# A first scatter pass for expert 0 alone, ahead of the full pass, in a fused attention and two-MoE kernel

## The chip, the cores and the metric

The kernel runs on one core of one Trainium2 chip. The metric is the device time of one execution in microseconds (us). The kernel before takes 1359.37 us, the median of three runs (1359.05 to 1359.9).

A core has five engines that run their own instruction streams: TensorE (PE) multiplies matrices, VectorE (DVE) and ScalarE (ACT) work on tiles elementwise, GpSimd (POOL) issues the indirect DMAs here, and SyncE (SP) issues the plain DMAs. "SPq" and "POOLq" in a profile are the parts of SP and POOL that issue DMAs. The core's 16 DMA engines move the data.

## The reference, cut to what matters

```python
def reference(**kwargs):
    attn_out = _attn_ref(...)          # windowed attention, 2 x 8 heads x 768 x 64
    x = attn_out.transpose(0, 2, 1, 3).reshape(1536, 512)
    x = _moe_ref(x=x, **moe_kwargs)    # every token through all 8 experts, soft weights
    return _moe2_ref(x=x, **moe2_kwargs)

def _moe2_ref(x, w_gate, w1, w2):
    cap = N // E                       # 1536 // 8 = 192
    logits = x @ w_gate
    for idx in np.argsort(-logits.flatten()):
        tok, e = idx // E, idx % E     # a token goes to the best expert that has room
        if assigned[tok] >= 0 or counts[e] >= cap: continue
        assigned[tok] = e; counts[e] += 1
    for e in range(E):
        mask = assigned == e           # exactly 192 tokens
        h = np.maximum(x[mask] @ w1[e], 0.0)
        out[mask] = h @ w2[e]
```

The case is about the passage from the first MoE to the second. Once the assignment is known, each expert of the second MoE needs its own 192 token rows, which lie scattered over the 1536 rows of the first MoE's result.

## The kernel before, in words

**Tokens.** The 1536 tokens stand in 12 tiles of 128. The first MoE's result lies in `acc[0]` to `acc[5]`, two tiles each. The last tiles to be finished are 10 and 11: their sums (`accl` in the profile) close only with the last matmuls of the first MoE (`make_g2`, L1163), while the routing is already known for all tokens.

**Routing to rows.** `pos[:, t]` says for each token of tile t which row it gets in the DRAM array `xs_d`: rows 0 to 191 are expert 0's, 192 to 383 expert 1's and so on. `scatter(t)` (L2056) writes a tile's 128 rows of 513 numbers there with an indirect DMA from POOL. Tiles 0 to 9 (NE = 10) are scattered as soon as the rows are known (L1950). Tiles 10 and 11 follow in `make_last_scatters` (L1955), after expert 0's rows were read.

**Fetch.** `make_rows` has SP read each expert's 192 rows back into `xs` (L2100): expert 0's once the first ten scatters have landed, the others' once all twelve have.

**Expert 0.** Its rows from tiles 10 and 11 are not in `xs_d` yet when it is read. They come by another way: DVE builds a one-hot table per tile (`hot`, from an IOTA named `slot` and the positions), and TensorE multiplies `accl` by it (`direct`, L2174), straight into a PSUM bank. Onto the same bank it adds the rows that were fetched, by fp32 matmuls with the identity (`move`, L2165). For the other experts the rows are turned by transposes (`tr`, L2150). ACT then copies the bank to `xe` in fp32r (the high part, L2154), DVE subtracts and keeps the low part (L2158).

**Steps.** The second MoE has 64 steps, eight for each expert (u = 0 to 3 blocks of 256 hidden columns, two halves each). A step is m1 (L2211 and L2213: four pairs of matmuls, hidden activations), a PSUM read by ACT and an add by DVE, the split `hs` into high and low part (ACT L2233, DVE L2237), and m2 (L2255 to L2264: five matmuls onto the expert's output banks). The weights arrive by SP in halves, `w1r` (L938) and `w2r` (L943), and are split into `w1hs`/`w1ls` and `w2hs`/`w2ls` (ACT L962, DVE L960). There are four weight slots, so expert 1's block u reuses the slot of expert 0's block.

**Order.** A list scheduler at build time fixes the order of instructions on each engine. A task has an engine, a planned duration, predecessors and a priority; among those that could start soon the one of lowest priority goes first. Where the planner sees TensorE idle, `warm` fills the gap with transposes of the identity (L206). Each engine then runs its list strictly in order, and waits where its next instruction is not ready.

Of the kernel before, what the change touches and what calls it, by code (L numbers as in the profile page):

```python
# [22 lines left out]
def tile_attention_moe_moe(ctx, tc, q, k, v, n_sink, window, wg1, w1a, w2a, wg2, w1b, w2b, out):  # L23
# [5 lines left out]
    P = 128  # L29
# [35 lines left out]
    class Task:  # L65
        __slots__ = ("alts", "fn", "deps", "prio", "acq", "rel", "left", "succ", "end", "eng", "closed", "name")
# [18 lines left out]
    class Sched:  # L85
# [11 lines left out]
        def task(self, eng, cost, fn, deps=(), prio=0.0, use=(), acq=None, rel=None, name=""):  # L97
            x = Task()
            x.name = name
            x.alts = [(eng, cost)] if isinstance(eng, str) else list(zip(eng, cost))  # L100
            x.fn, x.prio, x.acq, x.rel, x.succ, x.end, x.eng = fn, prio, acq, rel, [], None, None
# [109 lines left out]
        def emit(self, x, eng, t, cost):  # L211
# [14 lines left out]
            if len(x.alts) > 1:  # L226
                x.fn(eng)
            else:
                x.fn()
# [697 lines left out]
    def make_load(n):  # L927
# [18 lines left out]
        def load(k):  # L946
# [3 lines left out]
            return task("SP", 1.46, l2, deps=deps + [d1] + (SCT[NE - 1:NE] if 1 <= need - n_defer < 3 else []), prio=pr - 21, use=hs_[1:], name=f"raw{n}")  # L950
# [193 lines left out]
    def make_g2(s, hh_, hd, pr, what, jo=0, dyn=False):  # L1144
# [20 lines left out]
        for j in range(GT):  # L1165
            oh = [] if dyn else [OH_[jo + j]]
            for parts in ((0,), (1,), (2,)) if dyn else ((0, 1, 2),):
                y = task("PE", 0.2325 * len(parts), lambda j=j, parts=parts: g2(j, parts),
                         deps=hd + [LAST.get(("g2", jo + j)), FREE.get(f"o{jo + j}")] + w2t[f], prio=pr,
# [346 lines left out]
    def make_gate2():  # L1516
# [23 lines left out]
        def zero_rows(j):  # L1540
            nc.sync.dma_start(xs_d[j * P:(j + 1) * P, :], gp["zero"])
# [6 lines left out]
        for j in range(NT):  # L1548
            ZR.append(task("SP", 1.5, lambda j=j: zero_rows(j), deps=[x], prio=pr + 8.0 * j))
# [94 lines left out]
    def make_parts(s, g, fc, hh_, pr):  # L1644
# [8 lines left out]
        return a, task(("DVE", "POOL"), (0.43, PLO), lo, deps=[a], prio=pr, use=[hh_], name="hlo")  # L1653
# [3 lines left out]
    def make_deferred(q_):  # L1657
# [11 lines left out]
        a, b = make_parts(s, g, fc, hh_, pr - 32.5)  # L1669
        DEF.extend((a, b))  # L1670
        make_g2(s, hh_, [a, b], pr + 5.0, (LE, g, n, f, k == 0, k == 2 * NU - 1), dyn=True)
# [21 lines left out]
    def make_routing():  # L1693
# [256 lines left out]
        for t in range(NE):  # L1950
            SCT.append(task("POOL", 1.1, lambda t=t: scatter(t), deps=[place_, CB[t]] + ZR, prio=t, name="scatter"))
# [3 lines left out]
    def make_last_scatters():  # L1955
        for t in range(NE, NT):
            SCT.append(task("POOL", 1.1, lambda t=t: scatter(t), deps=[placed, CB[t]] + LDX[0], prio=t, name="scatter"))
# [96 lines left out]
    sc, SCT = [], []  # L2054

    def scatter(t):  # L2056
        nc.gpsimd.memset(spacer, 0.0)
        i = nc.gpsimd.indirect_dma_start(
            out=xs_d[:, :], out_offset=bass.IndirectOffsetOnAxis(ap=pos[:, t:t + 1], axis=0),
            in_=acc[t // GT][:, t % GT, :], in_offset=None)  # L2060
        for o in sc:
            tc.declare_no_dep(i.ins, o.ins, reason="distinct rows")
        sc.append(i)
# [11 lines left out]
    XS, XE, IDX, rkp, oh = {}, {}, {}, {}, {}  # L2075
# [15 lines left out]
    def make_rows(e, sw):  # L2091
# [5 lines left out]
        def ldx():  # L2097
            for n, (o, m) in enumerate(parts_of(e)):
                x = rkp["p"].tile([P, XW], F32, name=f"xs{n}", bufs=3)[:m]
                nc.sync.dma_start(x[:, :w], xs_d[e * cap + o:e * cap + o + m, :w])  # L2100
                XS[e, n] = x

        LDX[e].append(task("SP", 1.1, ldx, deps=SCT + [sw, placed], prio=v_two(8 * e - 26.0) - (500 if e == 0 else 0), use=[XSH[e]], name=f"xs{e}"))

    def make_tr(e):
# [14 lines left out]
        if e == 0:  # L2120
# [4 lines left out]
            ARR = [task("X", 4.0, lambda: None, deps=LDX[0], name="landed")]  # L2125
# [14 lines left out]
        for c2 in range(DC // 2):  # L2140
# [19 lines left out]
            def move(c2=c2, key=key):  # L2160
                p = bank[key][:, :2 * cap].rearrange("p (a b) -> p a b", a=2)
                for cc in range(2):
                    c = 2 * c2 + cc
                    for n, (o, m) in enumerate(parts):
                        nc.tensor.matmul(p[:, cc, o:o + m], XS[e, n][:, c * P:(c + 1) * P], ident[:m, :m],  # L2165
                                         start=False, stop=(cc == 1 and n == 1), skip_group_check=True)

            def direct(t, c2=c2, key=key):
                if c2 == 0 and t == NE:
                    XE[e] = rkp["p"].tile([P, DC, 2, cap], F32R, name="xe")  # L2170
# [251 lines left out]
```

## Time and profile before

| | |
|---|---|
| median of three runs | 1359.37 us (1359.05 to 1359.9) |
| the profiled execution | 1360.64 us |
| its span, first to last instruction | 1358.7 us |
| PE busy | 1348.2 us, 99% |
| DVE, ACT, POOL busy | 915.8, 607.2, 95.4 us |
| granted TensorE clock, mean | 0.998 of full speed |
| last matmuls of the first MoE | 1187.67 us |
| first m1 of the second MoE | 1196.22 us |

Times in the profile count from the first instruction of one profiled execution. That execution took 1360.64 us, 1.94 us longer than its span. Matmuls are pipelined: the start of the next one is the better mark than a duration, and "x4" after a row means four like it in a run. In square brackets stands how long the engine was idle just before, and what ended the wait.

### The profile page before, as it was taken

What the parts mean: (1) busy time and instruction counts of PE and PEld (TensorE: products, weight loads), DVE (VectorE), ACT (ScalarE), POOL (GpSimd) and SP (SyncE); (2) the same over time, 40 slices, a digit from 0 to 9 for tenths busy, and PEclk for the clock granted to TensorE, in tenths of its full rate; (3) what the DMA queues carried; (4) which work ended last, traced back from release to release, by engine and by line L of the source; (5) the groups of instructions that cost most, each with busy time, mean ns of one, the idle gap of its engine ahead of it and who ended that gap; (6) DMA issues with size and microseconds to landing.
All of it is one profiled execution on the core that took longest, in us unless ns stands there. A gap on an engine that the chain in (4) does not pass through costs nothing.

```text
span 1358.7 us, 22466 instructions
## 1 busy us (share of the span) xinstructions
PE 1348.2 (99%) x8288; PEld 1169.6 (86%) x8288; DVE 915.8 (67%) x2438; ACT 607.2 (45%) x1536; POOL 95.4 (7%) x246
## 2 busy tenths in 40 slices
PE   9999999999999999999999999999999999999997
PEld 7988888989989888899988899888887777788886
DVE  7877757865555555646364645459889868678885
ACT  7766653734333332424242433231133454367774
POOL 3111110000000000000000000000001013410111
PEclk9999999999999999999999999999999999999999
DMA  8331111202010101111020201064020011378873
GB/s 181 97 75 42 40 31 41 78 17 63 16 48 17 47 21 44 31 32 49 14 63 1 62 1 63 16 213 129 16 80 30 1 32 47 96 234 278 245 234 91
DMA packets 100036, 99.02 MB, mean 73 GB/s; under 512 B 42248, under 2 KB 76552, under 8 KB 99792
## 3 DMA queue, kind: packets, MB, share of 16 engines
q1 hardware_dynamic: 97936, 91.22, 22.9%
q0 software_dynamic: 1984, 6.30, 1.3%
q8 instruction: 67, 1.10, 0.3%
q14 instruction: 49, 0.40, 0.1%
HBM read 86.47 MB, written 11.04 MB: 72 GB/s over the span
## 4 chain that ended last, share of the span: by engine, by line
PE 96%; DMA 1%; DVE 1%; POOL 1%; issue 0%; ACT 0%; POOLq 0%; ACTq 0%; SPq 0%
PE hp L1381 16%; PE o L1470 12%; PE hp L1228 10%; PE o L1163 9%; PE side L1381 6%; PE av L1470 6%; PE side L1470 6%; PE hp L1132 5%; PE side L1163 2%; PE av L754 2%; PE av L1163 2%; PE side L731 1%; PE side L2211 1%; PE o L206 1%; PE hp L2211 1%; PE side L507 1%
## 5 line engine op out<-in xcount | busy, mean ns | idle before, releaser
L1439 ACT ACTIVATE hh<-c 128x256 fp32r<-128x256 f32 x180 | 74.8, 415 | 124.3 <-DVE c L1406 110.5
L1228 PE MATMUL hp<-xp,w1hs 128*128 128x512 f32 x384 | 120.7, 395 | 0.0
L1406 DVE TENSOR_TENSOR c<-hp,cp 128x256 f32<-128x256 f32 x120 | 50.9, 424 | 96.5 <-PE hp L1381 92.5
L1470 PE MATMUL o<-w2ls,hh 128*128 128x512 f32 x240 | 94.5, 394 | 0.0
L1470 PE MATMUL o<-w2hs,hl 128*128 128x512 f32 x240 | 94.5, 394 | 0.0
L1470 PE MATMUL o<-w2hs,hh 128*128 128x512 f32 x240 | 94.4, 393 | 0.0
L1381 PE MATMUL hp<-xp,w1hs 128*128 128x256 f32 x480 | 88.6, 282 | 0.0
L1228 PEld LDWEIGHTS hp<-xp,w1hs 128*128 128x128 f32 x384 | 69.5, 188 | 14.9
L1442 DVE SCALAR_TENSOR_TENSOR hl<-c,hh 128x256 fp32r<-128x256 f32 x180 | 74.5, 419 | 10.4 <-ACT hh L1439 7.9
L1381 PEld LDWEIGHTS hp<-xp,w1hs 128*128 128x128 f32 x480 | 76.8, 188 | 4.4
L1228 PE MATMUL hp<-xp,w1ls 128*128 128x512 f32 x192 | 75.8, 395 | 0.0
L1132 PE MATMUL hp<-xp,w1hs 128*128 128x256 f32 x384 | 75.5, 289 | 0.0
L1163 PE MATMUL o<-w2hs,hh 128*128 128x512 f32 x176 | 71.5, 406 | 0.0
L1439 ACT ACTIVATE hh<-hp 128x256 fp32r<-128x256 f32 x60 | 23.0, 384 | 107.4 <-PE hp L1381 107.4
L1163 PE MATMUL o<-w2hs,hl 128*128 128x512 f32 x176 | 69.6, 395 | 0.0
L1163 PE MATMUL o<-w2ls,hh 128*128 128x512 f32 x176 | 69.4, 394 | 0.0
L1398 ACT ACTIVATE cu<-hp 128x256 f32<-128x256 f32 x60 | 23.1, 385 | 103.1 <-PE hp L1381 103.0
L1381 PE MATMUL hp<-xp,w1ls 128*128 128x256 f32 x240 | 67.4, 281 | 0.0
L1442 DVE SCALAR_TENSOR_TENSOR hl<-hp,hh 128x256 fp32r<-128x256 f32 x60 | 25.5, 425 | 58.6 <-ACT hh L1439 58.3
L960 DVE TENSOR_TENSOR w1ls<-w1r,w1hs 128x512 fp32r<-128x512 f32 x84 | 56.8, 684 | 11.2 <-ACT w1hs L962 10.8
L1132 PEld LDWEIGHTS hp<-xp,w1hs 128*128 128x128 f32 x384 | 60.4, 189 | 2.5 <-DVE xp L787 0.2
L1248 ACT ACTIVATE hh<-hp 128x256 fp32r<-128x256 f32 x48 | 16.8, 383 | 98.0 <-PE hp L1228 96.5
(512 smaller groups left out, 3976.9 us busy)
## 6 DMA issues: line engine op xcount, KB each, us to landing
wr<-in_moe_w_dram SPq DMA_DIRECT2D x44, 512.0 KB
w1r<-in_moe_w_dram SPq DMA_DIRECT2D x42, 512.0 KB
w2r<-in_moe_w_dram SPq DMA_DIRECT2D x42, 512.0 KB
xs<-xs_d SPq DMA_DIRECT2D x14, 256.5 KB
xs_d<-zero SPq DMA_DIRECT2D x12, 256.5 KB
nk<-in_k_dram SPq DMA_DIRECT2D x12, 256.0 KB
nq<-in_q_dram SPq DMA_DIRECT2D x12, 256.0 KB
nv<-in_v_dram SPq DMA_DIRECT2D x12, 256.0 KB
```

What stands on the lines that cost most here:

```text
L754: nc.tensor.matmul(o[hh * D:(hh + 1) * D, hp, :], NAT["v", bl[j]][:, 2 * hp + hh, :], ET[t, hp][:, hh, j, :], start=(hp == 0 and z < 2), s ...
L960: (nc.gpsimd if eng == "POOL" else nc.vector).tensor_tensor(lo[:, c], r[:, c], f32(hi[:, c]), op=OP.subtract)
L1132: nc.tensor.matmul(p, a, b, start=(c == 0 and j == 0), stop=(c == DC - 1 and j == 2), skip_group_check=True)
L1163: nc.tensor.matmul(OUTP[g, j], a_, b_, start=(first and i == 0), stop=(last and i == 2), skip_group_check=True)
L1228: nc.tensor.matmul(HS[k, 0].rearrange("p a b -> p (a b)"), a, b, start=(c == 0 and j == 0), stop=(c == DC - 1 and j == 2), skip_group_chec ...
L1381: nc.tensor.matmul(st[bk], l_[:, c], r_[:, c], start=(start and c == 0 and j == 0), stop=(c == 1 and j == 2), skip_group_check=True)
L1398: act(st[key], st[bk], AF.Copy)
L1406: tt(st[out], st[bk], st[key], op=OP.add)
L1439: act(hh, st[key], AF.Relu)
L1442: nc.vector.scalar_tensor_tensor(HT[i, f, t][1], st[key], 0.0, f32(HT[i, f, t][0]), op0=OP.max, op1=OP.subtract)
L1470: nc.tensor.matmul(OUTP[g, j % GT], a_, b_, start=(first and f == 0 and z == 0), stop=(last and f == 1 and z == 2), skip_group_check=True)
L2211: nc.tensor.matmul(p[:, :2 * cap], h1[:, w], XE[e][:, c].rearrange("p s t -> p (s t)"), start=(c == 0), stop=False, skip_group_check=True)
```

## The change

Expert 0 gets a DRAM array of its own, `xs0_d` of 192 rows. POOL first scatters tiles 0 to 9 with a bound: rows of 192 and above are dropped, so that only expert 0's rows are written. Only then does the full pass over tiles 0 to 9 into `xs_d` follow, and tiles 10 and 11 after it, which no longer wait for a read. Expert 0's fetch waits for the first pass alone; the fetches of the other experts wait for the full pass as before.

On TensorE, expert 0's `direct` products keep banks of their own. ACT copies them to SBUF (`keep`), the rows fetched are turned by transposes instead of identity matmuls, DVE adds the two (`join`), and ACT and DVE make high and low part from the sum.

Smaller edits: two more zero writes for `xs0_d`; the early `w2r` loads that waited for the ten scatters now wait for the first pass; the last ten low-part subtractions of the first MoE (`hlo`) go to DVE only; the last two units of the first MoE finish tile 10 before tile 11 (`turn`); and the planner is told 3 us and 8 us for the arrival of expert 0's and expert 1's rows (`ARR`).

```diff
         def zero_rows(j):
-            nc.sync.dma_start(xs_d[j * P:(j + 1) * P, :], gp["zero"])
+            o = xs_d[j * P:(j + 1) * P, :] if j < NT else xs0_d[(j - NT) * (cap - P):(j - NT) * (cap - P) + P, :]
+            nc.sync.dma_start(o, gp["zero"])
...
         for t in range(NE):
-            SCT.append(task("POOL", 1.1, lambda t=t: scatter(t), deps=[place_, CB[t]] + ZR, prio=t, name="scatter"))
+            SC0.append(task("POOL", 1.1, lambda t=t: scatter(t, True), deps=[place_, CB[t]] + ZR, prio=t, name="scatter"))
+        for t in range(NE):
+            SCT.append(task("POOL", 1.1, lambda t=t: scatter(t), deps=[CB[t], SC0[-1]], prio=NT + t, name="scatter"))
...
         for t in range(NE, NT):
-            SCT.append(task("POOL", 1.1, lambda t=t: scatter(t), deps=[placed, CB[t]] + LDX[0], prio=t, name="scatter"))
+            SCT.append(task("POOL", 1.1, lambda t=t: scatter(t), deps=[placed, CB[t]] + SCT[:NE], prio=2 * NT + t, name="scatter"))
...
+        if first:
+            i = nc.gpsimd.indirect_dma_start(out=xs0_d[:, :], out_offset=at, in_=src, in_offset=None,
+                                             bounds_check=cap - 1, oob_is_err=False)
+        else:
+            i = nc.gpsimd.indirect_dma_start(out=xs_d[:, :], out_offset=at, in_=src, in_offset=None)
...
-                nc.sync.dma_start(x[:, :w], xs_d[e * cap + o:e * cap + o + m, :w])
+                nc.sync.dma_start(x[:, :w], (xs_d if e else xs0_d)[e * cap + o:e * cap + o + m, :w])
...
-        LDX[e].append(task("SP", 1.1, ldx, deps=SCT + [sw, placed], ...))
+        LDX[e].append(task("SP", 1.1, ldx, deps=(SCT if e else SC0) + [sw, placed], ...))
...
-            ARR = [task("X", 4.0, lambda: None, deps=LDX[0], name="landed")]
+            ARR = [task("X", 3.0, lambda: None, deps=LDX[0], name="landed")]
+        elif e == 1:
+            ARR = [task("X", 8.0, lambda: None, deps=LDX[1], name="landed")]
...
-            def move(c2=c2, key=key):
...
-                        nc.tensor.matmul(p[:, cc, o:o + m], XS[e, n][:, c * P:(c + 1) * P], ident[:m, :m],
-                                         start=False, stop=(cc == 1 and n == 1), skip_group_check=True)
...
+            def keep(c2=c2, key=kd):
+                XD[c2] = rkp["p"].tile([CA, DM], F32, name="ya")[:, :2 * cap].rearrange("p (a b) -> p a b", a=2)
+                act(XD[c2].rearrange("p a b -> p (a b)"), bank[key][:, :2 * cap], AF.Copy)
+
+            def join(c2=c2, key=key):
+                d = XD[c2].rearrange("p a b -> p (a b)")
+                tt(d, bank[key][:, :2 * cap], d, op=OP.add)
...
+                x = task("PE", 0.44, tr, deps=ARR + prev, prio=pr + MV, use=[XSH[e], XEH[e]], acq=key, name="trx0")
...
+                z = task("DVE", 0.56, join, deps=[x, y], prio=pr, use=[XEH[e]], rel=key, name="xd")
```

The order of instructions is the same up to the end of the first MoE, except for the two zero writes on SP. What moves from there on is shown at three places.

SP's queue at the passage, before: `xs_12912` and `xs_12914` are expert 0's rows, the next pairs of `xs` experts 1's and 2's, L2123 fetches expert 0's row numbers.

```order
L943 DMA w2r<-in_moe_w_dram 128x2x512 x2
L2100 DMA xs_12912<-xs_d 128x512
L2100 DMA xs_12914<-xs_d 64x512
L943 DMA w2r<-in_moe_w_dram 128x2x512 x2
L2100 DMA xs_12976<-xs_d 128x513
L2100 DMA xs_12978<-xs_d 128x513
...
L2100 DMA xs_13009<-xs_d 128x513
L2100 DMA xs_13011<-xs_d 128x513
L943 DMA w2r<-in_moe_w_dram 128x2x512
L938 DMA w1r<-in_moe_w_dram 128x4x256
```

The same place after the change (`xs_12937` and `xs_12939` are expert 0's rows, now of `xs0_d`, which the listing calls by the same name):

```order
L944 DMA w2r<-in_moe_w_dram 128x2x512 x2
L2110 DMA xs_12937<-xs_d 128x512
L2110 DMA xs_12939<-xs_d 64x512
L944 DMA w2r<-in_moe_w_dram 128x2x512 x2
L2110 DMA xs_13050<-xs_d 128x513
L2110 DMA xs_13052<-xs_d 128x513
...
L944 DMA w2r<-in_moe_w_dram 128x2x512
L2110 DMA xs_13105<-xs_d 128x513
L2110 DMA xs_13107<-xs_d 128x513
L939 DMA w1r<-in_moe_w_dram 128x4x256 x2
```

The queue keeps its order up to expert 1's rows; then one `w2r` goes ahead of expert 2's rows, and the same transfers as before stand ahead of the next `w1r`.

TensorE from the last matmuls of the first MoE to the first m1, before: `hp_12827` and `hp_12832` are the banks of tiles 10 and 11, `side_12945` and `side_12953` expert 0's rows.

```order
L1163 MATMUL hp_12827<-w2hs_127,hl 128x512
L1163 MATMUL hp_12832<-w2hs_127,hl 128x512
L206 MATMUL side_12934<-ident 128x128 x10
L2174 MATMUL side_12945<-hot_12901,accl_2967 128x192 x2
...
L2165 MATMUL side_12945<-ident,xs_12912 128x128
L2165 MATMUL side_12945<-ident,xs_12914 128x64
...
L206 MATMUL side_12981<-ident 128x128 x6
L2211 MATMUL o_12988<-xe,w1hs_120 128x384
...
L206 MATMUL side_12999<-ident 128x128 x7
```

And after (`hp_12851` is tile 11's bank; `side_12968` one of the two banks of `direct`, `side_12992` and `o_13000` those of the transposes):

```order
L1164 MATMUL hp_12851<-w2ls_128,hh 128x512
L1164 MATMUL hp_12851<-w2hs_127,hl 128x512
L2181 MATMUL side_12968<-hot_12941,accl_2968 128x192 x2
...
L2165 MATMUL side_12992<-ident,xs_12937 128x128
L2165 MATMUL side_12992<-ident,xs_12939 128x64
...
L2165 MATMUL o_13000<-ident,xs_12937 128x128
L2165 MATMUL o_13000<-ident,xs_12939 128x64
...
L207 MATMUL side_13017<-ident 128x128 x15
L2237 MATMUL o_13033<-xe,w1hs_120 128x384
```

The ten fillers ahead of `direct` are gone, and the 13 that stood around the first m1 pairs are 15 in one piece ahead of them.

TensorE at the second half of expert 0's third block (step 5), before: the `hp_13053` rows with `w2hs_117` are its m2, `av<-ident,xs` the second half of expert 1's transposes, and `w1hs_125` stands for the fourth block's weights (steps 6 and 7).

```order
L2255 MATMUL hp_13053<-w2hs_117,hs 128x512
L2256 MATMUL hp_13053<-w2hs_117,hs 128x512
L2257 MATMUL hp_13053<-w2ls_118,hs 128x512
L2263 MATMUL side_13061<-w2hs_117,hs 128x512
L2264 MATMUL side_13061<-w2ls_118,hs 64x512
L2150 MATMUL av<-ident,xs_12976 128x128
...
L2211 MATMUL o_13153<-xe,w1hs_125 128x384
L2213 MATMUL o_13153<-xe,w1ls_126 128x192
```

And after (`side_13251` with `w1hs_120` is expert 1's first m1, step 8):

```order
L2237 MATMUL hp_13223<-xe,w1hs_125 128x384
L2239 MATMUL hp_13223<-xe,w1ls_126 128x192
L2281 MATMUL side_13109<-w2hs_117,hs 128x512
L2282 MATMUL side_13109<-w2hs_117,hs 128x512
L2283 MATMUL side_13109<-w2ls_118,hs 128x512
L2289 MATMUL o_13118<-w2hs_117,hs 128x512
L2290 MATMUL o_13118<-w2ls_118,hs 64x512
L2237 MATMUL hp_13223<-xe,w1hs_125 128x384
L2239 MATMUL hp_13223<-xe,w1ls_126 128x192
L2237 MATMUL side_13251<-xe,w1hs_120 128x384
```

The m2 of step 5 moves from ahead of seven of the eight m1 pairs of steps 6 and 7 to behind all but the last of them, and all of expert 1's transposes now stand ahead of it.

## Rows read from the trace of the kernel before

**Rows 1.** The page's busy time of each engine.

```profile
PE 1348.2 (99%) x8288; PEld 1169.6 (86%) x8288; DVE 915.8 (67%) x2438; ACT 607.2 (45%) x1536; POOL 95.4 (7%) x246
```

**Rows 2.** Windows: stretch, length, busy PE, PEld, DVE, ACT, POOL, clock, DMA, GB/s.

```profile
1212.00:1340.00 128.00, 128.00 (x748) 113.56 (x747) 110.65 (x300) 98.93 (x238) 16.23 (x28) 1.00 0.78 244
```

**Rows 3.** Chain of waits, 1130 to 1210: start, us, engine, what.

```profile
1180.63 6.92 DMA xs_d<-accl,pos
...
1202.67 6.81 DMA w1r<-in_moe_w_dram
```

**Rows 4.** PE's timeline at the passage: start, us, operation, count, [idle before].

```profile
1188.14 1.25 PE L206 MATMUL side<-ident 128*128 128x128 f32 x10
1189.23 2.77 PE L2174 MATMUL side<-hot,accl 128*128 128x192 f32 x16
...
1192.89 2.77 PE L2165 MATMUL side<-ident,xs 64*128 64x64 f32 x14 [0.68 <-DMA xs<-xs_d]
...
1196.22 0.42 PE L2211 MATMUL o<-xe,w1hs 128*128 128x384 f32 x1
...
1198.17 0.36 PE L2211 MATMUL o<-xe,w1hs 128*128 128x384 f32 x1
```

**Rows 5.** SP's timeline of DMA issues.

```profile
1183.30 0.37 SPq L943 DMA_DIRECT2D w2r<-in_moe_w_dram  x1
1187.57 1.29 SPq L2100 DMA_DIRECT2D xs<-xs_d  x2
...
1198.41 0.81 SPq L2100 DMA_DIRECT2D xs<-xs_d  x2
1199.27 0.97 SPq L2123 DMA_DIRECT2D xs<-xs_d  x2
1200.29 1.06 SPq L2100 DMA_DIRECT2D xs<-xs_d  x2
...
1202.67 0.38 SPq L938 DMA_DIRECT2D w1r<-in_moe_w_dram  x1
```

**Rows 6.** POOL's timeline.

```profile
1168.16 1.17 POOL L2058 DMA_INDIRECT xs_d<-acc,pos  x1 [0.87 <-DVE rinc L1839]
...
1180.63 1.00 POOL L2058 DMA_INDIRECT xs_d<-accl,pos  x1 [0.22 <-issue]
...
1193.69 0.98 POOL L2058 DMA_INDIRECT xs_d<-accl,pos  x1 [11.71 <-DMA xs<-xs_d]
...
1194.97 0.96 POOL L2058 DMA_INDIRECT xs_d<-accl,pos  x1 [0.22 <-issue]
```

**Rows 7.** DMA by queue, 1181 to 1183.3: packets, MB, share of 16 engines.

```profile
q0 software_dynamic: 144, 0.47, 63.8%
```

**Rows 8.** DMA by queue, 1186 to 1187.6.

```profile
q1 hardware_dynamic: 157, 0.30, 84.8%
```

**Rows 9.** DMA by queue, 1203 to 1209.

```profile
q1 hardware_dynamic: 1139, 1.69, 92.1%
```

**Rows 10.** ACT's timeline.

```profile
1194.14 0.49 ACT L2154 ACTIVATE xe<-side 128x384 fp32r<-128x384 f32 x1 [4.65 <-PE side L2165]
...
1209.50 0.63 ACT L962 ACTIVATE w1hs<-w1r 128x512 fp32r<-128x512 f32 x1 [1.30 <-DMA w1r<-in_moe_w_dram]
1210.04 0.34 ACT L2233 ACTIVATE hs<-sm 128x192 fp32r<-128x192 f32 x1
```

**Rows 11.** DVE's timeline.

```profile
1194.66 0.56 DVE L2158 TENSOR_TENSOR xe<-side,xe 128x384 fp32r<-128x384 f32 x1 [3.95 <-ACT xe L2154]
```

**Rows 12.** PE's timeline around steps 5 to 8.

```profile
1211.11 0.50 PE L2256 MATMUL hp<-w2hs,hs 128*128 128x512 f32 x1 [0.17 <-DVE hs L2237]
...
1212.14 0.60 PE L2150 MATMUL av<-ident,xs 128*128 128x128 f32 x4
...
1214.55 0.36 PE L2211 MATMUL side<-xe,w1hs 128*128 128x384 f32 x1
...
1214.84 0.36 PE L2211 MATMUL side<-xe,w1hs 128*128 128x384 f32 x1
```

## What is predicted

> **What bounds the kernel now.** I read the busy times first. The reader is to see that TensorE is busy for 99% of the span and nothing else comes near [rows 1]. A change can therefore win only where TensorE stands or does work that is not needed, and in this kernel such work has a name: the fillers of L206. So I read TensorE's timeline at the passage next. Before the first m1 of the second MoE there are ten fillers from 1188.14, then the direct products, 16 identity matmuls on the fetched rows that start at 1192.89 after a wait for the fetch, six more fillers, two m1 pairs from 1196.22, seven fillers, and from 1198.17 on (step 1) there is no gap [rows 4]. So the passage, from 1188.14 to 1198.17, takes 10 us, of which the direct products and one step's m1 are wanted work.
>
> The chain of waits says what sets it: the tenth scatter, whose landing takes 6.92 us from POOL's issue at 1180.63, then the fetch of expert 0's rows, issued at 1187.57 [rows 3, 5]. The same chain names a second place, 15 us later: a `w1r` issued at 1202.67 that takes 6.81 us, and an ACT piece `w1hs` at 1209.50 that waits 1.30 us for it [rows 3, 10]. ACT's `hs` of step 5 stands behind that piece at 1210.04, and TensorE's second matmul of step 5's m2 waits for `hs` until 1211.11 [rows 10, 12]. That wait costs TensorE only 0.17 us, so before the change the weight stream is just in time. After it, from 1212 to 1340, TensorE is busy for all of 128 us at full clock [rows 2]. What counts is therefore when step 8 (expert 1's first m1) starts, 1214.55 before [rows 12]; from there both kernels do the same matmuls, and I carry the difference at step 8 to the end.
>
> **First term: expert 0 starts earlier.** POOL issues a scatter every 1.28 us (1193.69 to 1194.97) and the first at 1168.16 [rows 6]. Ten in a row end at about 1168.16 + 9 x 1.28 + 1.0 = 1180.7. How long after that they have landed no row shows, since no scatter before drops rows. Bounds: the last two, alone, end at 1195.93 and SP goes on at 1198.41, 2.5 us later; the tenth ends at 1181.63 and SP goes on at 1187.57, 5.9 later [rows 5, 6]. That gives 1183.2 to 1186.6 for the fetch, and not before 1183.7, as a `w2r` is issued at 1183.30 ahead of it. I take 1184.5, near the short end, since seven rows of eight are not written. The fetch took 5.3 us from issue to its first use (1187.57 to 1192.89) with little beside it; now that `w2r` runs beside it, 0.52 MB, 1.7 us at the rate of [rows 9] (1.69 MB in 92% of 6 us, 0.31 MB/us). It lands at about 1191.5 (1189.0 to 1193.6).
>
> Meanwhile TensorE goes from the first MoE straight into the direct products (2.8 us): tile 10 now closes six matmuls before tile 11, some 1.5 us by the pace of m2 (1211.11 to 1212.14 for four), so the ten fillers that covered the sum of both tiles are gone. They end near 1190.9. From the rows' landing the path is: four transposes 0.6, join 0.56 (priced as the DVE row of the same size), copy 0.49, low part 0.56, and 0.3 for the hand-overs [rows 10 to 12], 2.5 us in all: first m1 at 1194.0 and, without the seven fillers, step 1 at 1195.2 against 1198.17. Gain 2.9 (0.7 if the rows land at 1193.6, 3.5 if the direct products are the later of the two). The two `keep` copies lie on ACT while the rows are in flight and cost nothing; if the rows came first, they would cost 0.5. The two added zero writes stand in SP's queue ahead of all that is shown here and are read only at the passage; if a load there had no slack, 0.26 MB each would cost 0.9 us. The `hlo` on DVE alone are hidden by an engine that is busy for 67% [rows 1]; where one came late to the last matmuls, it would cost about its 0.6.
>
> **Second term: expert 1's rows are later.** POOL now issues 22 scatters without a pause: the last ends at about 1168.16 + 21 x 1.28 + 1.3 = 1196.4, against 1195.93 before. That half microsecond is not the point; what matters is what is in flight then. Before, the last two scatters were alone, and landed 2.5 us after POOL. Now twelve full ones run beside the fetch (0.39 MB) and three `w2r` (0.52 MB each). The scatters alone hold 64% of the DMA engines [rows 7], so 36% of the 13 us from 1183.4 to 1196.4 is free, 4.7 us. At the rate of [rows 9] the other transfers need 6.4 us, at the poorer rate of [rows 8] (0.30 MB in 85% of 1.6 us) 8.9. A backlog of 1.7 to 4.2 us is left when POOL is done, and the landing comes 4.2 to 6.7 us behind it. I take the middle, 5.4: expert 1's fetch is issued at X = 1201.8 against 1198.41.
>
> The next `w1r` stands on SP behind that fetch and the same transfers as before: experts 1's and 2's rows, the row numbers and one `w2r`. Before it landed 11.1 us after the fetch was issued (1198.41 to 1209.50), in which SP waited a little for a buffer; by SP's own issue times (0.81 + 0.97 + 1.06 + 0.37) it could go 3.2 us after the fetch and not 4.3, and land 10.1 after it [rows 5, 10]. Between these, 10.6: L = 1212.4. ACT's order is unchanged here, `w1hs` ahead of step 5's `hs`, and TensorE's second matmul of that m2 comes 1.6 us after L (1209.50 to 1211.11). The planner has moved this m2 behind seven of the eight m1 pairs of steps 6 and 7, so that behind the wait only the rest of the m2 (1211.11 to 1212.14, 1.03) and one pair (0.29) are left: step 8 at L + 2.9 = 1215.3, against 1214.55 [rows 12]. Without the wait, step 8 would come 16.2 us after step 1 as before (16.38 less 0.17), at 1211.4. So the wait takes back all of the 3.1 us and 0.7 more. TensorE stands for some 3.9 us at step 5's m2.
>
> The sum against the profiled execution's own time is 1360.64 + 0.7 = 1361.3. That execution lies 1.3 above the median, so in the terms of the runs it is **1360.1 us**.
>
> **A rule beside this.** The scatters' packets run until 1183.3 at 64% [rows 7], yet SP is released at 1187.57, just as the packets of the `w2r` of 1183.30 thin out [rows 5, 8]. The Trainium skill ("DMA: Bandwidth & Descriptors", section "Queues, rings and completion order") says that the write which signals a completion is strongly ordered: it lands only after every earlier write of that DMA engine, across its queues. The trace agrees. By that rule the first pass may be signalled only after the same `w2r`, at about 1187.5; step 1 would then start near 1197.5, and the end would not move, because it hangs on the second term.
>
> **Rivals.** *The gain is kept.* Step 8 comes at 1211.4 if L is 1208.5 or less, so if X is near 1198: the second pass lands 2 us behind POOL as two scatters alone did. For it: the three `w2r` may be through by 1193, and the last scatters then run alone again. Against: the tenth scatter's 5.9. Time: 1359.4 - 3.1 = 1356.3. Between, each us of X is a us of time, and the sign turns at X = 1201.1.
>
> *The second pass lands much later.* If the twelve scatters and the loads hold each other up beyond my backlog, as 22 in a row were never seen, X reaches 1204.7 (8.3 us behind POOL): L = 1215.3, step 8 at 1218.2, 3.6 slower, 1363.0. The one wait on `w1hs` decides it, slower by over 2.7 us from X = 1203.8 on. For it: [rows 3], a landing of 6.92 with one `w2r` beside it, where now there are three.
>
> *Dropped rows cost as much as written ones.* Then the first pass lands no sooner than before, 1187.5, expert 0 gains under 1 us, the `w2r` behind its fetch start later too, and the full pass only adds ten scatters: X about 1205, 1363.4.
>
> **How the numbers follow.** 0.2% is 2.7 us, about what a measurement can tell here. The forecast case, X from 1200 to 1203.5, has 0.54 and its own range 1358.3 to 1362.0. The gain kept has 0.23, the late second pass 0.16, the costly drops 0.07. Faster by over 0.2%: 0.23; within: 0.54; slower: 0.23. The range 1356.4 to 1363.2 holds all but the tails of the rivals.
>
> **What would show it.** Right: expert 0's fetch issued near 1184.5, direct products without fillers ahead, first m1 near 1194, step 1 near 1195.2; then expert 1's fetch near 1201.8, ACT's `w1hs` waiting for `w1r` until about 1212.4, TensorE idle for 3 to 4 us before the second matmul of step 5's m2, step 8 near 1215.3, and no gap behind it. Wrong: expert 1's fetch by 1199 and no such gap (the gain is kept), a fetch of expert 0 at 1187 (first term), or a new gap behind step 8, which this sum has at nothing.

## The result, and the profile after

The changed kernel takes 1369.23 us, the median of six runs (1367.88 to 1370.67), against 1359.3; the ratio is 1.0072 [1.0059, 1.0085]. Forecast was 1360.1 with a range to 1363.2: the change makes the kernel 9.9 us slower, and the time lies outside the range. The profiled execution took 1369.02 us, 8.4 more than that of before, which lay 1.3 above its median.

The busy times answer to [rows 1]: TensorE does the same work and is still at 99%.

```profile
PE 1348.4 (99%) x8271; PEld 1168.3 (85%) x8271; DVE 917.4 (67%) x2441; ACT 608.5 (45%) x1538; POOL 106.1 (8%) x265
```

So the loss must be a place where TensorE stands. The windows find it (columns as in [rows 2]):

```profile
1168.00:1185.40 17.40, 17.12 (x74) 13.28 (x73) 7.97 (x23) 4.39 (x10) 14.44 (x27) 1.00 0.19 66
1185.40:1200.30 14.90, 5.50 (x13) 3.66 (x14) 3.34 (x8) 2.91 (x6) 8.13 (x17) 0.66 0.79 187
1200.30:1212.00 11.70, 11.70 (x79) 10.77 (x78) 8.35 (x19) 6.58 (x16) 1.31 (x3) 1.00 0.82 209
1212.00:1226.00 14.00, 14.00 (x81) 12.15 (x80) 10.97 (x34) 9.27 (x25) 0.00 (x0) 1.00 0.78 242
1226.00:1350.00 124.00, 124.00 (x723) 109.92 (x722) 106.93 (x284) 95.45 (x229) 16.21 (x28) 1.00 0.79 243
```

One stretch, 1185.4 to 1200.3: TensorE works 5.5 of 14.9 us, at a mean granted clock of 0.66 of full speed. It is the end of the first MoE, before the passage that the forecast was about. From 1200.3 on there is no gap. TensorE's timeline there, and the passage, to be held against [rows 4]:

```profile
1184.72 0.63 PE L1164 MATMUL hp<-w2hs,hl 128*128 128x512 f32 x2
1189.37 0.50 PE L1164 MATMUL hp<-w2hs,hh 128*128 128x512 f32 x1 [4.02 <-ACT hh L1649]
1189.70 0.48 PE L1164 MATMUL hp<-w2ls,hh 128*128 128x512 f32 x1
1192.27 0.79 PE L1164 MATMUL hp<-w2hs,hl 128*128 128x512 f32 x1 [2.09 <-issue]
1196.40 0.79 PE L1164 MATMUL hp<-w2hs,hh 128*128 128x512 f32 x1 [3.34 <-ACT hh L1649]
...
1199.98 0.45 PE L1164 MATMUL hp<-w2hs,hl 128*128 128x512 f32 x1
1200.27 2.76 PE L2181 MATMUL side<-hot,accl 128*128 128x192 f32 x16
1202.87 0.94 PE L2165 MATMUL side<-ident,xs 128*128 128x128 f32 x4
1203.74 0.99 PE L2165 MATMUL o<-ident,xs 128*128 128x128 f32 x4
1204.66 1.86 PE L207 MATMUL side<-ident 128*128 128x128 f32 x15
1206.28 0.42 PE L2237 MATMUL o<-xe,w1hs 128*128 128x384 f32 x1
...
1207.48 0.36 PE L2237 MATMUL av<-xe,w1hs 128*128 128x384 f32 x1
...
1223.31 0.36 PE L2237 MATMUL side<-xe,w1hs 128*128 128x384 f32 x1
```

TensorE stands three times, 4.02 + 2.09 + 3.34 = 9.45 us, and the matmuls after that start every 0.43 us where before they took 0.23: half speed, the 1.2 GHz level (granted clock 0.50 from 1192.2 to 1196.4 and 0.53 from there to 1200.3, behind the idle times). The direct products come 11.0 later than before, without the ten fillers (1.1) that stood ahead of them; so the end of the first MoE comes 12.1 later. Step 1 is 9.3 later and step 8 8.8 later (1223.31 against 1214.55). The passage itself therefore gained 2.8 of the forecast 2.9, behind a loss that the forecast does not have.

What TensorE waits for is ACT's `hh`, the first and the third time, and DVE's `hl` in between (TensorE goes on at 1192.27, 0.06 us behind the end of `hl`). ACT and DVE in turn wait for something that the profile can't name:

```profile
1183.21 0.42 ACT L1649 ACTIVATE hh<-xp 128x256 fp32r<-128x256 f32 x1 [3.82 <-PE hp L1164]
1183.54 1.14 ACT L963 ACTIVATE w2hs<-w2r 128x512 fp32r<-128x512 f32 x2
1188.90 0.42 ACT L1649 ACTIVATE hh<-xp 128x256 fp32r<-128x256 f32 x1 [4.22 <-remote]
1195.94 0.42 ACT L1649 ACTIVATE hh<-xp 128x256 fp32r<-128x256 f32 x1 [6.62 <-remote]
```

```profile
1191.79 0.42 DVE L1652 TENSOR_TENSOR hl<-xp,hh 128x256 fp32r<-128x256 f32 x1 [6.32 <-remote]
```

"remote" means that no instruction on record ended when the wait did. The trace also keeps the moments at which an engine's semaphore rises, that is, at which its signal counts for the others. Over the rest of the span TensorE's rises come 0.01 to 0.02 us after the matmul that causes them. Here they do not. Which matmul a late rise belongs to can be told by e1 below: its TensorE, ACT and DVE run the same instructions in the same order as in the changed kernel, and none of its rises is late. In e1 the last `hh` goes on 0.04 us behind the end, at 1182.33, of the matmul that signals it:

```profile
1182.37 0.42 ACT L1649 ACTIVATE hh<-xp 128x256 fp32r<-128x256 f32 x1 [0.98 <-PE hp L1164]
```

In the changed kernel the same matmul ended at 1181.60, and the same `hh` starts at 1195.94. In this way (us from the span's start; on record, rises not being part of the views above):

```
matmul that signals ended    TensorE's semaphore rises    late by
after   1178.79              1183.19                       4.4
after   1180.19              1188.88                       8.7
after   1180.65              1191.70                      11.1
after   1181.60              1195.91                      14.3
after   1185.35              1196.11                      10.8
before  1178.05              1179.55                       1.5
before  1183 to 1340                                       0.01 to 0.02
```

The first and the fourth row come from the same `hh` in e1, the other rows of "after" from the order: as many rises as signals are on record here, and the last four rises come within 0.2 us. The row of 1179.55 comes from e17, which does with the kernel before what e1 does with the changed one. Held against the last matmul on record alone, as must be done where no such second kernel is at hand, the rise of 1188.88 looks 3.5 us late; such a figure is a lower bound.

ACT goes on at 1188.90 and 1195.94, each 0.02 to 0.03 behind a rise. So the waits are for signals of work that TensorE had done 9 and 14 us before. The rises of ACT, DVE and POOL that are on record are on time. POOL in these microseconds issues the full pass:

```profile
1180.61 1.13 POOL L2070 DMA_INDIRECT xs_d<-acc,pos  x1 [0.24 <-issue]
...
1192.59 0.96 POOL L2070 DMA_INDIRECT xs_d<-accl,pos  x1 [0.22 <-issue]
...
1199.12 1.16 POOL L2070 DMA_INDIRECT xs_d<-accl,pos  x1 [5.48 <-DVE accl L1180]
1201.50 1.16 POOL L2070 DMA_INDIRECT xs_d<-accl,pos  x1 [1.14 <-DVE accl L1180]
```

Its last two scatters stand behind the late `accl`, so expert 1's rows are late as well; SP's queue against [rows 5]:

```profile
1185.93 1.04 SPq L2110 DMA_DIRECT2D xs<-xs_d  x2
1199.47 3.35 SPq L944 DMA_DIRECT2D w2r<-in_moe_w_dram  x2
1207.14 0.82 SPq L2110 DMA_DIRECT2D xs<-xs_d  x2
```

X is 1207.14, against the forecast 1201.8. It costs nothing more, since TensorE itself is 9 us late by then: ACT's `w1hs` waits for no `w1r`.

### The profile page after: what moved, and what is told of

It reads as the page before. It is cut to its first block, busy times and chain, and to the rows that moved or that the text cites. A ratio compares the mean times of both kernels' runs of the same rounds, so it can differ in the third digit from the quotient of the medians.

```text
span 1367.1 us, 22455 instructions
## 1 busy us (share of the span) xinstructions
PE 1348.4 (99%) x8271; PEld 1168.3 (85%) x8271; DVE 917.4 (67%) x2441; ACT 608.5 (45%) x1538; POOL 106.1 (8%) x265
## 4 chain that ended last, share of the span: by engine, by line
PE 97%; another core or an unknown queue 1%; DVE 0%; SPq 0%; DMA 0%; ACT 0%; issue 0%; POOL 0%; POOLq 0%; ACTq 0%
PE hp L1382 16%; PE o L1471 12%; PE hp L1229 10%; PE o L1164 9%; PE side L1382 6%; PE av L1471 6%; PE side L1471 6%; PE hp L1133 5%; PE side L1164 2%; PE av L1164 2%; PE av L755 2%; PE hp L1164 2%; PE side L2237 1%; PE side L732 1%; PE hp L2237 1%; PE o L207 1%
## 5 line engine op out<-in xcount | busy, mean ns | idle before, releaser
L1229 PEld LDWEIGHTS hp<-xp,w1hs 128*128 128x128 f32 x384 | 69.5, 188 | 14.9
```

The source lines that it names most:

```text
L1229: nc.tensor.matmul(HS[k, 0].rearrange("p a b -> p (a b)"), a, b, start=(c == 0 and j == 0), stop=(c == DC - 1 and j == 2), skip_group_chec ...
```

## The experiments

Theories at the start: (A) the full pass's written rows crowd the DMA engines; (B) the mere issue of so many scatters in a row delays TensorE's signals; (C) one of the small edits (`hlo`, `turn`) makes the chain of the first MoE tight. The runs fell on chips 3, 10, 14 and 4 in turn (e1 to e4, e5 to e8 and e13 to e16, e9 to e12, e17 and e18), which turned out to matter; the kernel before takes 1359.72, 1359.40 (1359.25), 1360.09 and 1358.98 us on them. Times without an interval are of one run.

**e1, the full pass drops its rows.** In the full pass `bounds_check=0, oob_is_err=False`.

> The changed kernel, but the full pass drops every row except row 0: POOL issues the same 22 scatters, almost nothing is written by the last twelve, so experts 1 to 7 work on zeros and their rows are not put out. Three theories for the two stalls at the end of the first MoE (4.2 and 6.6 us in which ACT's hh waits, although TensorE's matmuls before it are long done). Issue theory: TensorE's signals come late because POOL issues so many indirect DMAs in a row, whatever they write: the stalls stay at 8 to 11 us, the time stays near 1369. Traffic theory: the written rows, the fetch and the weight loads on the DMA engines hold the signals up: no stall over 1 us, first MoE done near 1188, time 1356 to 1360. Order theory: the low-part subtractions on DVE alone and the turned order of the two tiles make ACT, DVE and TensorE wait on each other: stalls stay, 1369.

1357.35 us on chip 3. No wait in `hh`, no late signal. SP's fetches are where the gain kept would have them:

```profile
1183.81 0.92 SPq L2111 DMA_DIRECT2D xs<-xs_d  x2
...
1198.56 0.81 SPq L2111 DMA_DIRECT2D xs<-xs_d  x2
```

This seemed to settle (A): issue costs nothing, written rows some 12 us (1369.23 against 1357.35). It did not hold on another chip (e10). What the kernel leaves out at its end hardly matters: from the start of the last matmul to the end of the span it takes 6.9 us, e3 7.3.

**e2, the full pass planned behind the first MoE.** `deps=[CB[t], CB[NT - 1], SC0[-1]]`.

> The changed kernel, but the full pass waits for the last sum of the first MoE, so that only the ten scatters of the first pass run beside the first MoE. Issue and traffic theory: no stall over 1 us, first MoE done near 1187.5, step 1 near 1195; the full pass then runs from about 1189 to 1205, expert 1's fetch goes near 1208 and its weights behind it, time about 1364 to 1369. Order theory: both stalls stay, time over 1370.

1368.01 us, but the edit missed its aim: a dependency in the plan is an order and not a wait, and POOL began the full pass at 1181.89 all the same. No signal is late here. The planned order put three `w2r` and two `w1r` ahead of expert 1's fetch, the DMA engines were full (share 1.07 from 1188 to 1200), TensorE waited for expert 0's rows until 9.3 us after their issue, and X was 1209.14.

**e3, one pass and the rest of the change.** The scatters, waits and fetch as before; direct banks, transposes, join and small edits as after.

> All of the change but the first pass: tiles 0 to 9 are scattered once, in full, as before, expert 0's rows are fetched from the common array, and the last two scatters wait for that fetch; direct banks, transposes, join, the turned order and the low parts on DVE stay. Issue theory: ten in a row as before, no stall over 1 us; fetch near 1187.5, first m1 near 1195.4, step 8 near 1213, time 1357 to 1358.5. Traffic theory: the same. Order theory: the stalls stay, 1365 or more.

1357.25 us (1356.38 to 1359.78) against 1359.72: 0.9984 [0.9975, 0.9994]. TensorE, to be held against [rows 4]:

```profile
1187.71 2.76 PE L2179 MATMUL side<-hot,accl 128*128 128x192 f32 x16
1190.31 0.94 PE L2163 MATMUL side<-ident,xs 128*128 128x128 f32 x4
...
1192.10 1.86 PE L207 MATMUL side<-ident 128*128 128x128 f32 x15
1193.72 0.42 PE L2235 MATMUL o<-xe,w1hs 128*128 128x384 f32 x1
```

No fillers ahead of the direct products, step 1 at 1194.93: the gain of the passage without the first pass at all, with the fetch as late as 1186.51.

**e4, the small edits undone.** `("DVE", "POOL")` for all `hlo`, `turn=0`.

> The changed kernel without its two small edits at the end of the first MoE: the last ten low-part subtractions may go to POOL again and the two tiles end together. Issue and traffic theory: the stalls stay, 1366 to 1372. Order theory: they vanish, time 1357 to 1361.

1368.97 us, and a different picture: no wait in `hh`, no late signal, the first MoE ends at 1188.0. The loss lies 25 us later, in rows of ACT, TensorE and SP:

```profile
1206.81 0.81 SPq L2110 DMA_DIRECT2D xs<-xs_d  x2
```

```profile
1216.93 0.63 ACT L963 ACTIVATE w1hs<-w1r 128x512 fp32r<-128x512 f32 x1 [9.10 <-DMA w1r<-in_moe_w_dram]
```

```profile
1217.86 0.79 PE L2281 MATMUL o<-w2hs,hs 128*128 128x512 f32 x1 [5.58 <-ACT hs L2259]
```

This is the forecast's second term, only larger. The windows say why: the DMA engines have no free time for 15 us (next to last column).

```profile
1188.00:1193.00 5.00, 5.00 (x33) 4.30 (x31) 3.13 (x5) 0.63 (x2) 4.12 (x9) 1.00 1.05 225
1193.00:1198.00 5.00, 4.37 (x33) 3.87 (x34) 2.81 (x5) 2.35 (x6) 4.33 (x7) 1.00 1.00 262
1198.00:1203.00 5.00, 5.00 (x31) 4.46 (x30) 3.41 (x11) 3.39 (x9) 0.58 (x2) 1.00 0.99 235
...
1217.90:1230.00 12.10, 12.10 (x60) 10.54 (x61) 9.81 (x30) 8.50 (x20) 0.75 (x1) 0.82 0.74 241
```

After its wait TensorE runs at 0.82 of full speed for 12 us, another 2.2. Two different stalls thus give the same total; to tell whether the chip or the small edits choose between them took e5 to e11.

**e5, the changed kernel unaltered, and e6, the `w2r` tied to the full pass** (`SCT[NE - 1:NE]` for `SC0[NE - 1:NE]`), on chip 10.

> The changed kernel once more, unaltered. If the stalls at the end of the first MoE belong to it: ACT's hh waits 8 to 11 us in all there again, and the last two scatters are issued after 1199. If they came by chance in the one execution shown: no such wait, the last scatters near 1196, expert 1's fetch still near 1207, and the time still near 1369, because the late landing of the full pass alone sets it.

> The changed kernel with one part undone: the two early w2r loads wait for the tenth scatter of the full pass again, not for the first pass, and so leave the DMA engines to the scatters. Traffic theory: the full pass lands earlier by what these loads take, 3 to 5 us; expert 1's fetch near 1202 to 1204 and the time 1363 to 1367. Issue theory (22 indirect DMAs take their time by themselves): the fetch stays near 1207, time 1368 to 1371.

1367.94 and 1367.54 us. Both stand at the end of the first MoE, on late signals: up to 9.7 us in e5, where its `hh` is held against e1's, and up to 9.2 in e6 by the last matmul on record that signals. In e6 one `w2r` instead of two lies between the two fetches, and X stays (1206.39 against 1206.37): there the loads don't set it, the late `accl` does.

**e7, one pass without the small edits**, and **e8, `hlo` alone undone** in the changed kernel.

> The single pass with TensorE's part of the change alone: direct banks, copy, transposes and join, without the two small edits (low parts on DVE, tile 10 ahead of tile 11). If the gain of the single pass with all of it (some 2 us) is the shorter way from the fetch to the first m1, it stays: 1356.5 to 1358. If it is the filler time that the turned order saves, it goes: the ten fillers stand again, 1358.5 to 1360.

> The changed kernel with the low-part subtractions free to go to POOL again, but tile 10 still finished ahead of tile 11. If the stalls come from the subtractions on DVE alone, they vanish here; if from the turned order, they stay (8 to 11 us). Time 1367 to 1371 in both, since the late full pass sets it.

e7: 1359.62 (1358.88 to 1361.65) against 1359.40, 1.0003 [0.9993, 1.0012]. The ten fillers are back ahead of the direct products:

```profile
1188.20 1.25 PE L207 MATMUL side<-ident 128*128 128x128 f32 x10
1189.29 2.12 PE L2179 MATMUL side<-hot,accl 128*128 128x192 f32 x12
```

So banks and transposes alone gain nothing, and e3's gain needs the small edits. (The two ran on different chips; e12, below, is e3 on a third.) e8: 1368.47, signals late again, so `hlo` on DVE is not the cause. Nor does it remove the fillers: e8, with the turned order alone, has none ahead of the direct products, while e4, with neither edit, has ten.

**e9, e10, e11, e12: the changed kernel, e1, e4 and e3 again**, on chip 14.

> The changed kernel a third time, now beside the next two on one chip, because e4 (without the two small edits) ran on another chip than e5, e6 and e8 and alone of them showed no stall at the end of the first MoE. If the stall belongs to the kernel: it is here again, 6 us or more in all. If it depends on the chip: it is here when it is in e11, and absent when absent there. Time 1367 to 1370 either way.

> The full pass with every row but row 0 dropped, on the same chip as e9. Traffic theory: whatever e9 shows, no stall here, and 1356 to 1359. Issue theory: the same stall as e9, and a time over 1363.

> The changed kernel without its two small edits, on the same chip as e9. If the stall comes from these edits: none here, but ACT's w1hs waits some 9 us for its load and TensorE over 5 us behind it; if the chip decides: the same stall as in e9. Time 1367 to 1370.

> The single pass with all other parts of the change, once more and in more rounds: 1356.5 to 1358, faster than before by 1.5 to 3 us on this chip too. If its gain was only that of the other chip: within 1 us of before.

1369.60, 1365.89, 1369.34, and for e12 1358.71 (1357.18 to 1360.56) against 1360.09, 0.9991 [0.9982, 1.0000]. e4's program now has late signals and stands at the end of the first MoE: (C) falls, and the chip decides. And e1's program, whose full pass writes nothing, costs 8.5 us more here than on chip 3, while the kernel before differs by 0.4 between the two. TensorE of e10, for a result of DVE (`xe`) that is itself behind late signals (5.5 us late at 1198.14, by the same instruction in e1):

```profile
1195.16 3.28 PE L207 MATMUL side<-ident 128*128 128x128 f32 x15 [0.77 <-ACT ya L2188]
1202.17 0.67 PE L2238 MATMUL o<-xe,w1hs 128*128 128x384 f32 x1 [3.74 <-DVE xe L2198]
```

**e13, the full pass really waits** for the first MoE: POOL copies an element of the last `accl` into the spacer ahead of it.

> The changed kernel with a full pass that really waits: POOL reads one element of tile 11's last sum ahead of it. Late-signal cause: no stall at the end of the first MoE (under 2 us), step 1 near 1195 to 1197. Late-landing cause: the full pass starts near 1189.5 and ends near 1205, expert 1's fetch goes near 1208 to 1210, and TensorE waits for expert 1's weights instead: 1364 to 1369 all the same. If only the stall counted: 1358 to 1361.

1372.36 us on chip 10. The end of the first MoE has no wait now. The full pass runs from 1189 to 1205, and the late signals move with it, to 1205.7 to 1207.5 (by 4.2 us or more at the end), and TensorE stands at another matmul:

```profile
1209.05 0.79 PE L2284 MATMUL side<-w2hs,hs 128*128 128x512 f32 x1 [5.73 <-ACT hs L2262]
```

X is 1214.98. The delay belongs to the run of scatters, not to the place.

**e14 and e15, ten more scatters in the kernel before**, behind its first ten, into a spare array; in e14 their rows are dropped (`bounds_check=0`), in e15 written.

> The kernel before with ten more scatters behind its first ten, into a spare array, every row but row 0 dropped; nothing reads it. Late-signal cause by issue alone: TensorE or ACT waits 3 us or more near 1185 to 1198, 1362 to 1368. Late-landing cause by written rows: expert 1's fetch at 1199 to 1201 (POOL ends some 1 us later than before), 1359 to 1361.

> The same as e14 with all rows of the ten extra scatters written. Late-landing cause: the last two scatters land late, expert 1's fetch at 1205 to 1208, w1hs waits 6 us or more for its load, 1365 to 1370. Issue alone: the same time as e14.

1370.14 and 1368.65 us against 1359.25 on chip 10: ten dropped scatters cost 10.9 us, ten written ones 9.4. This is (B) by itself, with nothing else of the change. TensorE of e14, and the window around it:

```profile
1198.10 5.15 PE L2181 MATMUL side<-hot,accl 128*128 128x192 f32 x16 [6.30 <-DVE accl L1179]
```

```profile
1192.00:1196.00 4.00, 0.00 (x0) 0.00 (x0) 0.00 (x0) 0.85 (x2) 3.17 (x7) 0.99 0.40 132
```

From 1192 to 1196 TensorE and DVE do nothing, and the DMA engines are at 40%: no lack of bandwidth. The `accl` that TensorE waits for starts 0.02 us behind a rise of TensorE's own semaphore at 1197.27, 6.8 us late by the same instruction in e17.

**e16, one pass with the `w2r` behind expert 0's fetch** (`0 <= need - n_defer < 3`), an attempt at a better version.

> The single pass with the rest of the change, and one w2r more put behind expert 0's fetch, so that fewer bytes go beside the ten scatters. If the fetch waits for what shares the DMA engines with the scatters, it is issued 1 to 2 us earlier (near 1186) and the time falls to 1355.5 to 1357.5; if not, or if the weights then come late, 1358 to 1360.

1360.76 (1359.76 to 1362.77), 1.0011 [1.0002, 1.0021]. Expert 1's fetch goes at 1194.79, but the weight is missing a step later:

```profile
1201.34 0.63 ACT L963 ACTIVATE w2hs<-w2r 128x512 fp32r<-128x512 f32 x1 [3.78 <-DMA w2r<-in_moe_w_dram]
```

**e17, five dropped scatters in the kernel before, and e18, the same five with pauses** (twelve writes of the spacer ahead of each, one scatter in 2.8 us).

> The kernel before with five extra scatters behind its first ten, each the same as a scatter of the first ten but with a bound of 0 on the row number, so that it writes next to nothing, into a spare array; POOL issues 15 in a row, to about 1187.1 us, and the last two scatters of the kernel as before (they also wait for the five). Ten extra ones cost 10.9 us. If the signals of TensorE come late from about the twelfth scatter in a row on, as in the changed kernel (ACT's hh late by 4 to 7 us behind 1183), the time is 1362 to 1367 us with a wait of 2 to 5 us in hh or accl. If it takes more than 15 in a row, or on a chip where the signals are not late, the time is that of the kernel before, 1359 to 1360.

> As e17, but POOL does twelve small writes of the spacer ahead of each of the five extra scatters instead of one, so that it issues one every 2.3 to 2.6 us there instead of every 1.28. If the signals are late because POOL issues without a pause, the wait of e17 is gone or at most 1 us and the time is 1359 to 1361 us. If the number of scatters behind one another decides, whatever the pace, the wait stays at 2 to 5 us and the time at 1362 to 1367, or more, since the stretch lasts 6 us longer.

1358.81 and 1362.27 against 1358.98, on chip 4. No signal is late in either, so they don't tell pace from number; 15 in a row are free on this chip. e18 tests something else: its last two scatters come 4.3 us later than e17's, X is 1201.06 (1197.18 in e17), and

```profile
1210.78 0.63 ACT L962 ACTIVATE w1hs<-w1r 128x512 fp32r<-128x512 f32 x1 [2.24 <-DMA w1r<-in_moe_w_dram]
```

9.7 us behind X. With X 3.9 later than in e17 the time is 3.5 longer, but that is no measure of what a us of X costs: 1.07 us of TensorE's waits stand ahead of the direct products, for an `accl` that DVE takes up late, because its `hot` tables waited 4.75 us for the paused POOL; the two waits at step 5's m2, behind the late `w1r`, are 0.97 together.

**What the eighteen say together.** On chips 10 and 14 and in the first measurement, whose chip is not on record, TensorE's signals come late in all runs with twenty scatters or more in a row, also when their rows are dropped, and in e13 at the end of a run of twelve. In kernels with ten in a row the same chips show the beginning of it: 1.5 us in the kernel before (against e17) and 3.1 in e12 (against e3), and 0.45 in e7 and 0.43 in e16 as lower bounds by the last matmul on record that signals. The kernel before pays nothing for it that shows: 1359.40 and 1360.09 us on chips 10 and 14, 1359.72 and 1358.98 on 3 and 4. On chips 3 and 4 no rise is over 0.06 us late around the passage in any run. There the written rows fill the DMA engines and expert 1's rows are late (e4, e2); dropped ones are free (e1, e17). The changed kernel itself was not run on chip 3, and each chip but 10 was used at one time only, so that something else than the chip could stand behind the difference. Why one chip delays the signals and another does not, and from which scatter on, stays open; so does whether pauses would help. Where the signals are late the record also has holes: of POOL's rises from 1160 to 1205 it holds 10 of 18 in before and 14 of 27 in the changed kernel, against 28 of 28 in e4. All runs here were recorded, so whether the recording has a part in the delay can't be told from them.

## Why the prediction was wrong, by its steps

**What bounds the kernel.** Right: a us that TensorE stands is a us of time, and after the passage there is no gap.

**First term, expert 0 earlier by 2.9 us.** The size came out, 2.8 us in the changed kernel and 3.2 in e3, but not for the reason given, and so by luck. The first pass lands at the short end: in e1 POOL ends its tenth scatter at 1181.37 and the fetch goes at 1183.81, 2.4 later (forecast 1184.5). In the changed kernel it goes at 1185.93, because the `w2r` ahead of it in SP's queue, issued at 1185.51, waited for its slot, which DVE freed late behind the late `hh` of 1183.21. The Trainium skill ("DMA: Bandwidth & Descriptors", section "Queues, rings and completion order") has a completion land only after every earlier write of that DMA engine; I had drawn from it that the fetch could be held to 1187.5. It was not: of the `w2r` of 1181.85 only 0.03 MB were moved by 1183.8, so nearly all its writes were not earlier ones, and e1 speaks neither for the rule nor against it. But the fetch was not what the passage waited for. e3 has it at 1186.51 and still gains 3.2 at step 1 (1194.93); e1, with the fetch 2.7 us earlier, has step 1 at 1196.26. What gains is the order: tile 10 closed first, so that the ten fillers go (e3 against e7, and e8 for the turned order alone). That order is already another one in the last matmuls of the first MoE, and one low-part subtraction moves from POOL to DVE there, so it is not, as said under the change, the same up to the end of the first MoE. The part that I priced as a detail of 1.5 us was all that the change is worth in these runs, and the two passes were not needed for it.

**"The `hlo` on DVE alone are hidden."** Nothing speaks against it: e8 and e5 differ by 0.5 us, one run each, both with the long stall.

**Second term, expert 1 later.** This is the step that failed. It says that POOL "now issues 22 scatters without a pause" and that this "half microsecond is not the point; what matters is what is in flight then". Issue was priced at POOL's own time, 1.28 us each, hidden as long as nobody waits for POOL. The runs show a second price: on chips 10 and 14 and in the first measurement the issue itself holds up TensorE's signals, by up to 14.3 us, and so the engines that wait for them (ACT's `hh`, DVE's `hl` and `accl`). e14 measures it at 10.9 us, in one run, for ten scatters that write next to nothing. It falls on the last matmuls of the first MoE, where TensorE has nothing else to do. The trace of before held a sign that I didn't read: rises 0.10, 0.36 and 0.32 us behind the last matmul on record that signals, at 1179 to 1182.6, under its ten scatters (1.5 us, as e17 later showed), and none like it in the rest of the passage.

**The backlog, where the signals are on time.** Also too small. e4 has X at 1206.81, 5.0 behind the forecast: 2.1 because POOL ended later (1198.50 for 1196.4; about half of this is e4's own, which gives a subtraction back to POOL, since e1 ends at 1197.46), 2.9 because the landing came 8.3 us behind it and not 5.4. I let the loads run in the 36% that scatters leave free [rows 7]. e4's DMA engines are full from 1183 to 1203; by queue (scatters, then loads; packets, MB, share):

```profile
q0 software_dynamic: 923, 3.05, 51.7%
q1 hardware_dynamic: 1030, 1.95, 46.3%
```

The scatters take 10.3 us of all 16 engines, where 64% of 13 us had made 8.3, and the loads the other 9.3, at 0.21 MB/us where [rows 9] had 0.31. Beside scatters a load takes half as long again. From X on the sum held in the main: L is X + 10.1 (10.6 forecast), the wait falls on step 5's m2 as forecast, 5.6 us for 3.9. The half clock behind it, 2.2 us, was not in the sum.

**The rivals.** "The second pass lands much later" named the mechanism that e4 shows on chip 3, where the landing also comes 8.3 us behind POOL; its 1363.0 was too low, with X taken at 1204.7 and no clock. "Dropped rows cost as much as written ones" had 0.07 and the wrong mechanism: they land early, but on chip 10 they cost as much by being issued (e14, e15). "The gain is kept" happens when the full pass writes nothing, on chip 3 (e1, 1357.35 for 1356.3).

**The range.** Its upper end was the sum of transfer terms. A new regime, 22 of something of which ten had been seen, was bounded only along the one resource I had thought of.

## What to carry to other kernels

Before lengthening a run of indirect DMAs, look in the trace at whether other engines' semaphores already rise late under the present run; a us or two that costs nothing there can be the start of a steep curve. And where a second run has the same instructions with its signals on time, read the delay from the same wait in both; the last matmul before the rise gives only a lower bound. Price such a run three ways: POOL's time, the DMA engines' time beside everything else that moves then, and the waits of other engines for signals. And take a bundled change apart: here the single pass with direct banks, transposes, join and turned order is faster than both kernels, by 2.5 us on chip 3 (e3) and 1.4 on chip 14 (e12, with an interval that reaches to no gain), while with the first pass, the change's main part, the time on chip 14 is 10.9 us longer (e9 against e12).

## What was not expected of the hardware

- TensorE's semaphore rises 0.01 to 0.02 us after a matmul, but up to 14.3 us after it late in a run of twenty scatters (the changed kernel; 9.7 in e5 and e9, 6.8 in e14). The rises of ACT, DVE and POOL do not, as far as they are on record.
- It goes with the chip: the same program took 1357.35 us on one and 1365.89 on another (e1, e10), whose times for the kernel before are 0.4 apart.
- A scatter whose rows are all dropped takes POOL as long as a written one (mostly 0.97 us, one in 1.28; e1).
- A wait ended by "remote" was here a signal of the core's own TensorE, too late to be matched with its matmul.
